# Routing of a slot mixture with phi as the stationary operand, four batch rows on the column groups, and slot sums from 32-row tiles

## The chip, the cores and the metric

One core of one Trainium2 chip runs the whole program. The metric is the device time of one execution in microseconds (us). Matrix products run on TensorE (PE; its weight loads are listed apart as PEld), elementwise work and reductions on VectorE (DVE), ScalarE (ACT) and GpSimd (POOL), and transfers are issued by SyncE (SP) for the most part.

## The reference

A gated delta rule over 768 tokens, for 4 batch rows and 8 heads of 48, is followed by a soft mixture over 32 slots. Its output, laid out as x of 3072 tokens by 384, is what the second part reads:

```python
logits = x @ phi                                  # 3072 x 32
d = np.exp(logits - logits.max(0, keepdims=True))
d /= d.sum(0, keepdims=True) + 1e-09              # over the tokens
slot_input = d.T @ x                              # 32 x 384
...
for e in range(E):                                # 8 experts, 4 slots each
    h = np.maximum(slot_input[e] @ w1[e], 0.0)
    slot_out[e] = h @ w2[e]
...
c = np.exp(logits - logits.max(1, keepdims=True))
c /= c.sum(1, keepdims=True) + 1e-09              # over the slots
return c @ slot_out
```

## The kernel before, in words

Tokens go in 24 chunks of 32. Four chunks are a group (index n, 6 groups), and a chunk has eight units: one batch row b (4) and one half g of the heads (2). A unit lies on the 128 partitions as four heads of 32 tokens each.

For each group, `norm` (L177) normalises the keys, `prep` (L204) transposes keys and queries and makes the small products, and `invert` (L240) inverts a triangular matrix for all 128 blocks of the group at once. The inversion is a strict chain on DVE: 31 steps of a product (L264) and a subtraction (L267). It starts when `lb` has come back from DRAM and POOL has scaled it (L252), and its result goes out through DRAM (L272) and comes back as weights `TT` (L282).

`chunk` (L298) is the recurrence: R = V - Kn S (products L310, difference L314), the inverse times R (L324, scaled on DVE in L329), the state's update (L340, L345) and the output Y (L354, L359, copied by ACT in L362).

`route(n, Yn)` (L370) takes a finished group through the mixture's first half. Its steps are

- `logits(b)`, for each batch row: four transposes of Y (L379), a copy by ACT to `yT` (L381), four accumulated products with `yT` (96 x 128) stationary and `phi` (96 x 32) moving (L385), and a copy to `lg` (L387);
- `over_slots`: the softmax over the slots, kept in `Call`;
- `maximum`: the running maximum over the tokens, by a transpose (L407), reductions, and a product that spreads it over the partitions (L415), then the exponential `d`;
- `sums`: the running sum of the exponentials, and the rescaling of both running sums;
- `repeat`: `d` spread over the four heads of a unit by four products with `sel` (L443), copied by ACT to `dr` (L448);
- `slots(c)`, for each chunk: POOL masks `dr` into `db` (L453, one instruction for each batch row), four products with Y stationary (128 x 96) and `db` moving (128 x 128) (L458), and an addition to `sacc` (L464).

These steps are handed to the next group's chunks: the first two chunks of group n carry `prep` of group n + 1, the last two carry `invert` of group n + 1 and `route` of group n - 1, in pieces between the chunk's own products (`Fill`, `merge`). A scheduler then sets the final order on each engine, and each engine keeps its order strictly. A matrix product in 32-bit floats shows as two records in the trace, a transpose as one.

After the last group its routing runs alone (`drain(routing)`, L529), and then the experts: `first` (L557, w1 stationary, `sacc` moving), `second` (L568, w2 moving), and the output (L588).

Of the kernel before, what the change touches and what calls it, by code (L numbers as in the profile page):

```python
# [16 lines left out]
def kernel(  # L17
# [85 lines left out]
    # the same by blocks: partition 32 h + 8 c + u of a group of chunks  # L103
# [30 lines left out]
    sel = cpool.tile([P, GC, 4, C], F32, name="sel")  # L134
    for h in range(4):
        nc.gpsimd.tensor_copy(sel[:, :, h, :], ident.rearrange("p (c t) -> p c t", t=C))
    ones = cpool.tile([P, 1], F32, name="ones")
    nc.vector.memset(ones, 1.0)
# [65 lines left out]
    def prep(n, c):  # L204
        """Of a chunk: Kn and Q transposed, strict_lower(Q Kn^T) and Kn Kn^T (both transposed)."""
# [34 lines left out]
    def invert(n):  # L240
        """(I + L)^-1 transposed: tt[block][k][i] = T[i, k], a block on each partition."""
# [34 lines left out]
    def near(cc):  # L276
        """Of the next chunk: its inverse as weights, and Kn spread by heads."""
# [87 lines left out]
    Call = cpool.tile([P, NG, B, NSL], F32, name="Call")  # L365
    dsum = cpool.tile([P, NSL], F32, name="dsum")
    sacc = cpool.tile([GD, 4, NSL], F32, name="sacc")
    mrun = cpool.tile([NSL, 1], F32, name="mrun")
    mB = {}

    def route(n, Yn):
# [30 lines left out]
        def maximum():  # L402
            # the running maximum over the tokens, on every partition
            cm = small.tile([P, NSL], F32, name="cm", tag="cm")
            nc.vector.tensor_reduce(cm, lg.rearrange("p b s -> p s b"), axis=AX.X, op=ALU.max)
            pm = pt([NSL, P])
            nc.tensor.transpose(pm, cm, ident)  # L407
            if n == 0:
                nc.vector.tensor_reduce(mrun, pm, axis=AX.X, op=ALU.max)
            else:  # L410
                m1 = small.tile([NSL, 1], F32, name="m1", tag="m1")
                nc.vector.tensor_reduce(m1, pm, axis=AX.X, op=ALU.max)
                nc.vector.tensor_tensor(mrun, mrun, m1, op=ALU.max)
            pmb = pt([P, NSL])
            nc.tensor.matmul(pmb, lhsT=mrun.broadcast_to([NSL, P]), rhs=ident[0:NSL, 0:NSL],  # L415
                             start=True, stop=True)
            mB[n] = small.tile([P, NSL], F32, name="mB", tag="mB")
            nc.vector.tensor_copy(mB[n], pmb)
            nc.vector.tensor_tensor(d, lg, mB[n].unsqueeze(1).broadcast_to([P, B, NSL]),
# [3 lines left out]
        def sums():  # L423
            if n == 0:
                nc.vector.tensor_reduce(dsum, d.rearrange("p b s -> p s b"), axis=AX.X,
                                        op=ALU.add)
                return
            al = small.tile([P, NSL], F32, name="al", tag="al")
            nc.vector.tensor_tensor(al, mB.pop(n - 1), mB[n], op=ALU.subtract)
            nc.scalar.activation(al, al, ACT.Exp)  # L430
# [192 lines left out]
```

## Time and profile before

| | |
|---|---|
| median of 3 runs | 919.21 us (918.97 to 921.51) |
| span of the profiled execution | 919.5 us |
| PE busy | 679.9 us, 74% of the span, 8324 instructions |
| PEld busy | 565.6 us |
| DVE busy | 299.4 us, 33% |
| POOL busy | 192.9 us, 21% |
| ACT busy | 101.3 us, 11% |
| mean granted clock of TensorE | 0.701 of full speed |

The profiled execution's own time is listed only as its span, 0.3 us above the median. Busy times are unions, so products that run beside each other count once. The page's line for the granted clock shows full speed up to 277 us, but the same products take as long there as later at half speed: that line is to be trusted from the first recorded change on.

### The profile page before, as it was taken

The numbers are of one execution on the slowest core, as the hardware profiler recorded it, in microseconds if no ns is written. First come the engines' busy times: TensorE is split into PE (matmuls) and PEld (weight loads), VectorE is DVE, ScalarE is ACT, GpSimd is POOL, SyncE is SP. The second block draws the span as 40 slices with busy tenths as digits, with TensorE's granted clock in tenths as the row PEclk, the third lists the DMA queues.
The fourth block names the chain that finished last, engine by engine and source line by source line (L and its number), as shares of the span: only waits on it lengthen the run. The fifth ranks groups of instructions, "written<-read, shape, count | busy, mean of one in ns | idle before, by whom it ended". The sixth has DMA issues, their size and how long they took to land.

```text
span 919.5 us, 19108 instructions
## 1 busy us (share of the span) xinstructions
PE 679.9 (74%) x8324; PEld 565.6 (62%) x8324; DVE 299.4 (33%) x816; ACT 101.3 (11%) x223; POOL 192.9 (21%) x347
## 2 busy tenths in 40 slices
PE   1706569069990799807998069996499799999998
PEld 1504569058880688706888058885398696765754
DVE  3267112942139421394213942226421100000011
ACT  0303000021120211102111021111000110000001
POOL 7231213131251213412134111351210200000000
PEclk9999999999995555755557555565555567667765
DMA  6240763023310242102321021000100099990013
GB/s 118 37 85 26 133 115 72 1 52 55 75 20 0 58 70 55 20 0 58 69 55 19 0 58 32 25 2 0 35 13 1 1 266 211 237 231 16 1 60 146
DMA packets 148019, 58.12 MB, mean 63 GB/s; under 512 B 131968, under 2 KB 143328, under 8 KB 147936
## 3 DMA queue, kind: packets, MB, share of 16 engines
q1 hardware_dynamic: 141888, 55.87, 27.9%
q10 hardware_dynamic: 5664, 0.94, 0.6%
q8 instruction: 65, 1.06, 0.5%
q0 software_dynamic: 384, 0.10, 0.1%
q14 instruction: 18, 0.15, 0.1%
HBM read 45.86 MB, written 11.01 MB: 62 GB/s over the span
## 4 chain that ended last, share of the span: by engine, by line
PE 64%; DVE 17%; DMA 6%; POOL 4%; SPq 3%; ACT 3%; issue 2%; ACTq 0%; DVEq 0%; POOLq 0%
PE ph L557 9%; PE psW L324 8%; PE psY L359 7%; DVE pr L264 7%; PE pso L568 6%; PE psS L340 6%; DVE tt L267 6%; PE pt L215 5%; PE pt L385 5%; PE pt L458 3%; PE pout L588 3%; PE psR L310 2%; PE pt L230 2%; PE psY L354 2%; PE pt L379 2%; SPq L77 2%
## 5 line engine op out<-in xcount | busy, mean ns | idle before, releaser
L215 PE MATMUL pt<-ident,Ks 128*128 128x128 f32 x96 | 42.1, 438 | 167.9 <-POOL Ks L199 158.7
L291 POOL TENSOR_TENSOR KX<-Ks,hm 128x192 f32<-128x192 f32 x184 | 91.0, 531 | 354.0 <-PE psS L340 264.4
L215 PEld LDWEIGHTS pt<-ident,Ks 128*128 128x128 f32 x96 | 20.8, 216 | 173.9 <-POOL Ks L199 159.6
L324 PE MATMUL psW<-R,TT 128*128 128x48 f32 x384 | 86.6, 396 | 34.4 <-DMA TT<-td 31.2
L324 PEld LDWEIGHTS psW<-R,TT 128*128 128x128 f32 x384 | 81.1, 311 | 39.4 <-DMA TT<-td 19.1
L557 PEld LDWEIGHTS ph<-sacc,w1t 96*128 96x128 f32 x512 | 87.8, 272 | 3.8 <-issue 3.8
L557 PE MATMUL ph<-sacc,w1t 96*128 96x4 f32 x512 | 88.1, 310 | 0.0
L359 PE MATMUL psY<-U,AT 128*128 128x48 f32 x384 | 83.9, 393 | 0.0
L264 DVE TENSOR_TENSOR pr<-tt,lb 128x31 f32<-128x31 f32 (+15 forms) x186 | 76.7, 413 | 16.2 <-POOL lb L252 11.0
L359 PEld LDWEIGHTS psY<-U,AT 128*128 128x128 f32 x384 | 78.2, 306 | 3.4
L267 DVE TENSOR_TENSOR tt<-tt,pr 128x31 f32<-128x31 f32 (+15 forms) x186 | 73.3, 394 | 5.2
L340 PE MATMUL psS<-U,KX 128*48 128x48 f32 x1472 | 69.8, 271 | 0.0
L340 PEld LDWEIGHTS psS<-U,KX 128*48 128x48 f32 x1472 | 60.8, 181 | 6.3 <-issue 1.7
L568 PE MATMUL pso<-w2t,hx 128*32 128x384 f32 x128 | 58.5, 627 | 1.7 <-DVE hx L561 1.7
L329 DVE TENSOR_TENSOR U<-psW,bta 128x192 f32<-128x192 f32 x48 | 17.2, 358 | 113.4 <-PE psW L324 113.4
L345 DVE TENSOR_TENSOR S<-S,psS 112x384 f32<-112x384 f32 x46 | 25.5, 554 | 87.6 <-PE psS L340 87.3
L233 DVE TENSOR_TENSOR AT<-pt,bdm 128x512 f32<-128x512 f32 x48 | 31.9, 688 | 62.1 <-ACT Lc L232 59.0
L385 PE MATMUL pt<-phi,yT 96*128 96x32 f32 x192 | 45.1, 398 | 6.0 <-ACT yT L381 5.1
L230 PE MATMUL pt<-KQ 48*32 48x64 f32 x1536 | 47.5, 310 | 1.9
L385 PEld LDWEIGHTS pt<-phi,yT 96*128 96x128 f32 x192 | 42.0, 323 | 10.5 <-ACT yT L381 9.1
L561 DVE TENSOR_SCALAR hx<-ph 128x32 f32<-128x32 f32 x8 | 1.5, 192 | 141.0 <-PE ph L557 141.0
L354 PE MATMUL psY<-S,KQ 48*32 48x48 f32 x1536 | 46.1, 265 | 0.1
(107 smaller groups left out, 698.9 us busy)
## 6 DMA issues: line engine op xcount, KB each, us to landing
w1t<-in_moe_w_dram SPq DMA_DIRECT2D x16, 768.0 KB
w2t<-in_moe_w_dram SPq DMA_DIRECT2D x8, 1536.0 KB
Ks<-in_k_dram SPq DMA_DIRECT2D x96, 48.0 KB
V<-in_v_dram SPq DMA_DIRECT2D x96, 48.0 KB
out_dram<-ob SPq DMA_DIRECT2D x24, 192.0 KB
Qs<-in_q_dram SPq DMA_DIRECT2D x80, 48.0 KB
ld<-Lc SPq DMA_DIRECT2D x24, 128.0 KB
lb<-ld SPq DMA_DIRECT2D x6, 512.0 KB
```

Source lines behind the costliest of these rows:

```text
L215: nc.tensor.transpose(tp[:, i, a, :], src[:, c, b * G:(b + 1) * G, :].rearrange("p g d -> p (g d)"), ident)
L230: nc.tensor.matmul(pg[rh, b], lhsT=KQ[cc][r, b, 0, rh], rhs=KQ[cc][r, b, :, rh], start=True, stop=True, skip_group_check=True)
L264: nc.vector.tensor_tensor(prv, tt[:, 0:m, j:j + 1].broadcast_to([P, m, w]), lb[:, j, j + 1:C].unsqueeze(1).broadcast_to([P, m, w]), op=ALU ...
L267: nc.vector.tensor_tensor(tt[:, 0:m, j + 1:C], tt[:, 0:m, j + 1:C], prv, op=ALU.subtract)
L291: nc.gpsimd.tensor_tensor(KX[cc][:, g, b], kn[:, b].unsqueeze(1).broadcast_to([P, 4, D]), hm.unsqueeze(2).broadcast_to([P, 4, D]), op=ALU. ...
L324: nc.tensor.matmul(pw[:, i, g, :], lhsT=T[:, (2 * hf + i) * G + g].rearrange("p h t -> p (h t)"), rhs=Rs[hf][:, i, g, :], start=True, stop ...
L340: nc.tensor.matmul(psS[DP * g:DP * g + D, i, h, :], lhsT=kx[:, g, 2 * hf + i, h, :], rhs=Us[hf][:, i, g, :], start=True, stop=True, skip_g ...
L354: nc.tensor.matmul(py[C * h:C * h + C, b, :], lhsT=kq[r, b, 1, C * h:C * h + C], rhs=old[b // 2][r, b % 2, h, :], start=(b == 0), stop=Fal ...
L359: nc.tensor.matmul(py[:, b, :], lhsT=at[:, g, b].rearrange("p h t -> p (h t)"), rhs=Us[b // 2][:, b % 2, g, :], start=False, stop=True, sk ...
L385: nc.tensor.matmul(pl, lhsT=yT[:, h].rearrange("p c t -> p (c t)"), rhs=phi[:, h, :], start=(h == 0), stop=(h == 3))
L557: nc.tensor.matmul(st["ph"][:, t, :], lhsT=w1t[e][:, h, t * P:(t + 1) * P], rhs=sacc[:, h, sl], start=(h == 0), stop=(h == 3))
L568: nc.tensor.matmul(pso, lhsT=hx[:, e, t, :], rhs=w2t[e][:, t, :], start=(e == 0 and t == 0), stop=(e == E - 1 and t == NFC - 1))
```

## The change

The routing is written anew. `turn(b)` does the transposes and the copy to `yT`, which now holds all four batch rows. One step `logits` follows: `phi` (96 x 32) is stationary, `yT` of one batch row and head (96 x 128) moves, and batch row b writes to partitions 32 b to 32 b + 31; a copy by ACT and one transpose bring the result back to tokens on the partitions. `maximum` makes the running maximum on all 128 partitions (four copies of the 32 slots), and with it the factor `al`, one number for each partition. `repeat` uses slices of the identity, 16 products with 32 columns of weights. `slots(c)` needs no masked copy: for each batch row and head, `dr` (32 x 32) of the head's own 32 partitions is stationary and Y of these partitions moves, with a column of ones behind its 96 columns, so that column 96 of `sacc` is the sum of the exponentials. `sums` and `sel` are gone; the two buffers of Y have four more columns, set to one at the start. Behind the last routing, `sacc` is transposed once to `sT` for the experts.

```diff
-        def logits(b):
+        def turn(b):
+            if b == 0:
+                st["yT"] = wk.tile([GD, B, 4, GC, C], F32, name="yT", tag="yT", bufs=1)
             py = pt([GD, GC, P])
             for c in range(GC):
-                nc.tensor.transpose(py[:, c, :], Yn[:, c, b, :], ident)
-            yT = wk.tile([GD, 4, GC, C], F32, name="yT", tag="yT")
-            nc.scalar.activation(yT.rearrange("p h c t -> p c h t"),
+                nc.tensor.transpose(py[:, c, :], Yn[:, c, b, 0:GD], ident)
+            nc.scalar.activation(st["yT"][:, b].rearrange("p h c t -> p c h t"),
                                  py.rearrange("p c (h t) -> p c h t", h=4), ACT.Copy)
-            pl = pt([P, NSL])
+
+        def logits():
+            pl = pt([P, P])
             for h in range(4):
-                nc.tensor.matmul(pl, lhsT=yT[:, h].rearrange("p c t -> p (c t)"),
-                                 rhs=phi[:, h, :], start=(h == 0), stop=(h == 3))
-            nc.vector.tensor_copy(lg[:, b, :], pl)
+                for b in range(B):
+                    nc.tensor.matmul(pl[C * b:C * b + C], lhsT=phi[:, h, :],
+                                     rhs=st["yT"][:, b, h].rearrange("p c t -> p (c t)"),
+                                     start=(h == 0), stop=(h == 3), skip_group_check=True)
+            lT = wk.tile([P, P], F32, name="lT", tag="lT", bufs=1)
+            nc.scalar.activation(lT, pl, ACT.Copy)
+            pq = pt([P, P])
+            nc.tensor.transpose(pq, lT, ident)
+            nc.vector.tensor_copy(lg.rearrange("p b s -> p (b s)"), pq)
...
         def maximum():
...
-            nc.tensor.transpose(pm, cm, ident)
+            nc.tensor.transpose(pm, cm.rearrange("p h s -> p (h s)"), ident)
...
+                nc.vector.tensor_tensor(al, mrun, m1, op=ALU.subtract)
+                nc.scalar.activation(al, al, ACT.Exp)
...
-            nc.vector.tensor_tensor(d, lg, mB[n].unsqueeze(1).broadcast_to([P, B, NSL]),
+            nc.vector.tensor_tensor(d, lg, pmb.unsqueeze(1).broadcast_to([P, B, NSL]),
                                     op=ALU.subtract)
...
-        def sums():
...
         def repeat():
             pd = pt([P, GC, B, NSL])
             for c in range(GC):
-                nc.tensor.matmul(pd[:, c].rearrange("p b s -> p (b s)"),
-                                 lhsT=sel[:, c].rearrange("p h t -> p (h t)"),
-                                 rhs=d.rearrange("p b s -> p (b s)"), start=True, stop=True,
-                                 skip_group_check=True)
+                for h in range(4):
+                    nc.tensor.matmul(pd[C * h:C * h + C, c].rearrange("p b s -> p (b s)"),
+                                     lhsT=ident[:, C * c:C * c + C],
+                                     rhs=d.rearrange("p b s -> p (b s)"), start=True, stop=True,
+                                     skip_group_check=True)
...
         def slots(c):
-            db = wk.tile([P, B, 4, NSL], F32, name="db", tag="db")
+            pa = pt([P, GD + 1])
             for b in range(B):
-                nc.gpsimd.tensor_tensor(
-                    db[:, b], st["dr"][:, c, b].unsqueeze(1).broadcast_to([P, 4, NSL]),
-                    hm.unsqueeze(2).broadcast_to([P, 4, NSL]), op=ALU.mult)
-            pa = pt([GD, 4, NSL])
-            for b in range(B):
-                nc.tensor.matmul(pa.rearrange("p h s -> p (h s)"), lhsT=Yn[:, c, b, :],
-                                 rhs=db[:, b].rearrange("p h s -> p (h s)"),
-                                 start=(b == 0), stop=(b == B - 1))
+                for h in range(4):
+                    r = slice(C * h, C * h + C)
+                    nc.tensor.matmul(pa[r], lhsT=st["dr"][r, c, b, :], rhs=Yn[r, c, b, 0:GD + 1],
+                                     start=(b == 0), stop=(b == B - 1), skip_group_check=True)
             if n == 0 and c == 0:
                 nc.vector.tensor_copy(sacc, pa)
+            elif c == 0:
+                nc.vector.scalar_tensor_tensor(sacc, sacc, st["al"], pa, op0=ALU.mult,
+                                               op1=ALU.add)
             else:
                 nc.vector.tensor_tensor(sacc, sacc, pa, op=ALU.add)
...
+    Ys = [wk.tile([P, GC, B, GD + 4], F32, name=f"Y{i}", bufs=1) for i in range(2)]
+    for t in Ys:
+        nc.gpsimd.memset(t[:, :, :, GD:GD + 4], 1.0)
...
+    pst = pt([GD, P])
+    nc.tensor.transpose(pst, sacc[:, 0:GD], ident)
+    sT = cpool.tile([GD, 4, NSL], F32, name="sT")
+    nc.vector.tensor_copy(sT.rearrange("p h s -> p (h s)"), pst)
```

The order on the engines moves as follows. First, PE in the third chunk of a middle group, before (L340 is the state's update of the third chunk, L354 and L359 its output):

```order
L340 MATMUL psS<-U,KX 48x48
L385 MATMUL pt<-phi,yT 128x32 x4
L379 MATMUL pt<-ident,Y 96x128 x4
L340 MATMUL psS<-U,KX 48x48 x13
L385 MATMUL pt<-phi,yT 128x32 x4
L340 MATMUL psS<-U,KX 48x48 x2
L379 MATMUL pt<-ident,Y 96x128 x4
L354 MATMUL psY<-S,KQ 32x48 x8
L340 MATMUL psS<-U,KX 48x48 x7
L385 MATMUL pt<-phi,yT 128x32 x4
L340 MATMUL psS<-U,KX 48x48 x9
```

and in the changed kernel, where L335 is the state's update, L375 the transposes, L384 the logits and L390 the transpose behind them:

```order
L335 MATMUL psS<-U,KX 48x48 x16
L375 MATMUL pt<-ident,Y_629 96x128 x4
L384 MATMUL pt<-yT,phi 32x128 x3
L335 MATMUL psS<-U,KX 48x48 x7
L384 MATMUL pt<-yT,phi 32x128 x13
L335 MATMUL psS<-U,KX 48x48 x8
L390 MATMUL pt<-ident,lT 128x128
L335 MATMUL psS<-U,KX 48x48
```

The logits of the four batch rows, spread over the chunk before, stand together, in two pieces. From the first transpose to the fourth chunk's first product the order before lists 38 rows, the changed one 32.

Second, PE from the routing's maximum to the fourth chunk (L324), before (L415 spreads the maximum, L443 repeats, L458 sums the slots):

```order
L415 MATMUL pt<-ident,mrun 128x32
L310 MATMUL psR<-S,KQ 32x48 x15
L354 MATMUL psY<-S,KQ 32x48 x22
L443 MATMUL pt<-d,sel 128x128 x4
L354 MATMUL psY<-S,KQ 32x48 x7
L458 MATMUL pt<-db,Y 96x128 x16
L324 MATMUL psW<-R,TT_213 128x48 x8
```

and in the changed kernel (L426 spreads, L437 repeats, L449 sums, L319 begins the fourth chunk):

```order
L349 MATMUL psY<-S,KQ 32x48 x28
L426 MATMUL pt<-ident,mrun 128x32
L349 MATMUL psY<-S,KQ 32x48 x3
L437 MATMUL pt<-d,ident 32x128 x16
L449 MATMUL pt<-Y_629,dr 32x97 x64
L319 MATMUL psW<-R,TT_206 128x48 x8
```

Less of the chunk's own work stands between the spreading and the repetition, and none between the repetition and the sums. The elimination steps follow behind the fourth chunk on DVE in both orders.

Third, DVE in the last group's inversion, where the routing of the group before it is threaded through the elimination steps, before (L464 adds the slot sums):

```order
L464 TENSOR_TENSOR sacc<-sacc,pt 96x128
L267 TENSOR_TENSOR tt<-tt,pr 128x19x13
L264 TENSOR_TENSOR pr<-tt,lb 128x240
L464 TENSOR_TENSOR sacc<-sacc,pt 96x128
L267 TENSOR_TENSOR tt<-tt,pr 128x20x12
L264 TENSOR_TENSOR pr<-tt,lb 128x231
L464 TENSOR_TENSOR sacc<-sacc,pt 96x128
```

and in the changed kernel:

```order
L454 SCALAR_TENSOR_TENSOR sacc<-sacc,al,pt 128x97
L259 TENSOR_TENSOR pr<-tt,lb 128x240
L262 TENSOR_TENSOR tt<-tt,pr 128x20x12
L457 TENSOR_TENSOR sacc<-sacc,pt 128x97
L259 TENSOR_TENSOR pr<-tt,lb 128x231
L262 TENSOR_TENSOR tt<-tt,pr 128x21x11
L457 TENSOR_TENSOR sacc<-sacc,pt 128x97
```

The additions stand at the same elimination steps. Ahead of them the four copies of the logits have become one, further down among the steps.

## Rows read from the trace of the kernel before

**Rows 1.** The page's chain of waits, by engine and by line.

```profile
PE 64%; DVE 17%; DMA 6%; POOL 4%; SPq 3%; ACT 3%; issue 2%; ACTq 0%; DVEq 0%; POOLq 0%
PE ph L557 9%; PE psW L324 8%; PE psY L359 7%; DVE pr L264 7%; PE pso L568 6%; PE psS L340 6%; DVE tt L267 6%; PE pt L215 5%; PE pt L385 5%; PE pt L458 3%; PE pout L588 3%; PE psR L310 2%; PE pt L230 2%; PE psY L354 2%; PE pt L379 2%; SPq L77 2%
```

**Rows 2.** Timeline of PE, 384 to 505 us: start, duration, instruction, wait ahead.

```profile
419.02 0.47 PE L215 MATMUL pt<-ident,Ks 128*128 128x128 f32 x1 [29.49 <-POOL Ks L199]
```

**Rows 3.** Timeline of DVE, the same stretch.

```profile
389.24 1.29 DVE L264 TENSOR_TENSOR pr<-tt,lb 128x31 f32<-128x31 f32 x1
...
419.32 0.21 DVE L267 TENSOR_TENSOR tt<-tt,pr 128x31 f32<-128x31 f32 x1
...
504.64 1.29 DVE L264 TENSOR_TENSOR pr<-tt,lb 128x31 f32<-128x31 f32 x1
```

**Rows 4.** Timeline of POOL, the same stretch.

```profile
495.73 1.91 POOL L252 TENSOR_TENSOR lb<-lb,bb 128x1024 f32<-128x1024 f32 x1
```

**Rows 5.** Timeline of PE, 440 to 505 us.

```profile
440.08 0.60 PE L310 MATMUL psR<-S,KQ 48*32 48x48 f32 x32
440.42 0.73 PE L230 MATMUL pt<-KQ 48*32 48x64 f32 x16
...
446.09 1.88 PE L230 MATMUL pt<-KQ 48*32 48x64 f32 x60
...
454.17 3.65 PE L359 MATMUL psY<-U,AT 128*128 128x48 f32 x16
...
473.37 0.40 PE L340 MATMUL psS<-U,KX 128*48 128x48 f32 x4
473.70 1.09 PE L379 MATMUL pt<-ident,Y 128*96 128x128 f32 x4
...
475.20 0.87 PE L340 MATMUL psS<-U,KX 128*48 128x48 f32 x14
476.00 1.92 PE L385 MATMUL pt<-phi,yT 96*128 96x32 f32 x8
477.85 1.04 PE L340 MATMUL psS<-U,KX 128*48 128x48 f32 x18
...
487.16 2.08 PE L443 MATMUL pt<-d,sel 128*128 128x128 f32 x8
489.17 0.54 PE L354 MATMUL psY<-S,KQ 48*32 48x48 f32 x14
490.46 6.58 PE L458 MATMUL pt<-db,Y 128*96 128x128 f32 x32 [0.76 <-POOL db L453]
496.88 0.99 PE L324 MATMUL psW<-R,TT 128*128 128x48 f32 x8
...
500.20 1.99 PE L359 MATMUL psY<-U,AT 128*128 128x48 f32 x16
```

**Rows 6.** Windows of PE: us, busy (records), granted clock, DMA share, GB/s.

```profile
496.00:497.00 1.00, 1.00 (x10) 0.83 0.00 0
...
736.00:738.00 2.00, 1.77 (x18) 1.00 0.28 25
...
742.00:744.00 2.00, 2.00 (x12) 0.52 1.06 399
```

**Rows 7.** Timeline of DVE, 617 to 656 us, the last inversion.

```profile
626.03 0.19 DVE L387 COPY lg<-pt 128x32 f32<-128x32 f32 x1 [0.67 <-PE pt L385]
...
633.11 0.19 DVE L387 COPY lg<-pt 128x32 f32<-128x32 f32 x1 [2.19 <-PE pt L385]
...
643.86 0.28 DVE L464 TENSOR_TENSOR sacc<-sacc,pt 96x128 f32<-96x128 f32 x1 [2.37 <-PE pt L458]
...
648.89 0.28 DVE L464 TENSOR_TENSOR sacc<-sacc,pt 96x128 f32<-96x128 f32 x1 [0.81 <-PE pt L458]
```

**Rows 8.** Timeline of PE, 700 to 742 us, the last routing.

```profile
714.55 1.92 PE L385 MATMUL pt<-phi,yT 96*128 96x32 f32 x8 [0.74 <-ACT yT L381]
...
730.41 6.09 PE L458 MATMUL pt<-db,Y 128*96 128x128 f32 x32 [1.23 <-POOL db L453]
```

More of the change, by code (lines that the diff above doesn't have):

```diff
@@ L133 @@
     nc.vector.tensor_tensor(bdm, bdm, hm.unsqueeze(2).broadcast_to([P, 4, C]), op=ALU.mult)
[L134 to L138, printed above, removed]
     bta = cpool.tile([P, NCH, U], F32, name="bta")
@@ L365 @@
     Call = cpool.tile([P, NG, B, NSL], F32, name="Call")
[L366 to L369, printed above, removed]
+    sacc = cpool.tile([P, GD + 1], F32, name="sacc")
+    mrun = cpool.tile([P, 1], F32, name="mrun")
     def route(n, Yn):
@@ L410, in maximum @@
             else:
-                m1 = small.tile([NSL, 1], F32, name="m1", tag="m1")
+                m1 = small.tile([P, 1], F32, name="m1", tag="m1")
+                al = st["al"] = small.tile([P, 1], F32, name="al", tag="al")
                 nc.vector.tensor_reduce(m1, pm, axis=AX.X, op=ALU.max)
-                nc.vector.tensor_tensor(mrun, mrun, m1, op=ALU.max)
+                nc.vector.tensor_tensor(m1, mrun, m1, op=ALU.max)
+                nc.vector.tensor_tensor(al, mrun, m1, op=ALU.subtract)
+                nc.scalar.activation(al, al, ACT.Exp)
+                nc.vector.tensor_copy(mrun, m1)
             pmb = pt([P, NSL])
[L415 to L418, printed above, removed]
-            nc.vector.tensor_tensor(d, lg, mB[n].unsqueeze(1).broadcast_to([P, B, NSL]),
+            nc.tensor.matmul(pmb, lhsT=mrun[0:NSL].broadcast_to([NSL, P]),
+                             rhs=ident[0:NSL, 0:NSL], start=True, stop=True)
+            nc.vector.tensor_tensor(d, lg, pmb.unsqueeze(1).broadcast_to([P, B, NSL]),
                                     op=ALU.subtract)
             nc.scalar.activation(d, d, ACT.Exp)
-        def sums():
[L424 to L430, printed above, removed]
-            ds_ = small.tile([P, NSL], F32, name="ds_", tag="ds_")
-            nc.vector.tensor_reduce(ds_, d.rearrange("p b s -> p s b"), axis=AX.X, op=ALU.add)
-            nc.vector.tensor_tensor(dsum, dsum, al, op=ALU.mult)
-            nc.vector.tensor_tensor(dsum, dsum, ds_, op=ALU.add)
-            nc.vector.tensor_tensor(sacc, sacc,
-                                    al[0:GD].unsqueeze(1).broadcast_to([GD, 4, NSL]),
-                                    op=ALU.mult)
         def repeat():
@@ L450, in slots @@
         def slots(c):
-            db = wk.tile([P, B, 4, NSL], F32, name="db", tag="db")
+            pa = pt([P, GD + 1])
             for b in range(B):
-                nc.gpsimd.tensor_tensor(
-                    db[:, b], st["dr"][:, c, b].unsqueeze(1).broadcast_to([P, 4, NSL]),
-                    hm.unsqueeze(2).broadcast_to([P, 4, NSL]), op=ALU.mult)
-            pa = pt([GD, 4, NSL])
-            for b in range(B):
-                nc.tensor.matmul(pa.rearrange("p h s -> p (h s)"), lhsT=Yn[:, c, b, :],
-                                 rhs=db[:, b].rearrange("p h s -> p (h s)"),
-                                 start=(b == 0), stop=(b == B - 1))
+                for h in range(4):
+                    r = slice(C * h, C * h + C)
+                    nc.tensor.matmul(pa[r], lhsT=st["dr"][r, c, b, :], rhs=Yn[r, c, b, 0:GD + 1],
+                                     start=(b == 0), stop=(b == B - 1), skip_group_check=True)
             if n == 0 and c == 0:
                 nc.vector.tensor_copy(sacc, pa)
+            elif c == 0:
+                nc.vector.scalar_tensor_tensor(sacc, sacc, st["al"], pa, op0=ALU.mult,
+                                               op1=ALU.add)
             else:
                 nc.vector.tensor_tensor(sacc, sacc, pa, op=ALU.add)
-        return ([lambda b=b: logits(b) for b in range(B)] + [over_slots, maximum, sums, repeat]
+        return ([lambda b=b: turn(b) for b in range(B)] + [logits, over_slots, maximum, repeat]
                 + [lambda c=c: slots(c) for c in range(GC)])
@@ L537 @@
         load_w2(e, wp2, 5)
-    pd = pt([NSL, 1])
-    nc.tensor.matmul(pd, lhsT=dsum, rhs=ones, start=True, stop=True)
     rd = cpool.tile([NSL, 1], F32, name="rd")
-    nc.vector.tensor_scalar(rd, pd, 1e-9, None, op0=ALU.add)
+    nc.vector.tensor_scalar(rd, sacc[0:NSL, GD:GD + 1], 1e-9, None, op0=ALU.add)
+    pst = pt([GD, P])
+    nc.tensor.transpose(pst, sacc[:, 0:GD], ident)
+    sT = cpool.tile([GD, 4, NSL], F32, name="sT")
+    nc.vector.tensor_copy(sT.rearrange("p h s -> p (h s)"), pst)
     nc.vector.reciprocal(rd, rd)
@@ L557, in product @@
                 nc.tensor.matmul(st["ph"][:, t, :], lhsT=w1t[e][:, h, t * P:(t + 1) * P],
-                                 rhs=sacc[:, h, sl], start=(h == 0), stop=(h == 3))
+                                 rhs=sT[:, h, sl], start=(h == 0), stop=(h == 3))
         def relu():
```

11 lines of the change are left out of this document (7 added, 4 removed).

## The prediction

> **What bounds the kernel now.** I read the chain of waits first [rows 1]: two thirds of it are PE, and DVE's part is nearly all the inversion (L264, L267). The timelines show how the two alternate. In a middle group, PE stands still for 29.49 us until the keys are normalised [rows 2]. In that time DVE runs the inversion's steps, from 389.24 to 419.32 us [rows 3], with the normalisation queued among them. The next inversion starts at 504.64, 115.4 us after the one before. So a period is 30 us of DVE, and 85 us in which PE works through four chunks, the next group's `prep` and the routing, strictly in its order. When does the inversion start? Its input `lb` is ready on POOL at 495.73 + 1.91 = 497.64 us [rows 4], 7.0 us ahead of its first step. It waits for its place in DVE's queue, behind the differences R that follow PE's fourth chunk. What PE saves in the routing therefore moves the inversion forward, one for one, up to those 7 us (and `lb` stands behind the masks L453 on POOL, which go away).
>
> This holds four times (routing of groups 0 to 3). The routing of group 4 runs beside the last inversion, the routing of group 5 alone: six calls in all, with different worth.
>
> **The unit prices.** PE runs at half its clock in most of this; the prices are for that. A product of 48 x 32 weights with 64 columns moving, four of them on the four column groups, comes every 31 ns per record (1.88 us for 60), so 0.49 ns per moving column [rows 5]. That gives 62 ns per record for 128 columns and 47 for 97; I take 60 and 45, since the last record's tail is in the 1.88. The two row groups of L310 even run beside each other: its 32 records have started within 0.34 us [rows 5].
>
> **The four calls on the path, part by part** (a call is one group's routing):
>
> - Transposes and their copies: the same 16, nothing.
> - Logits: four blocks of 8 records, 1.85 us each (476.00 to 477.85) [rows 5], 7.2 us with the shorter ones. Now 16 products, 32 records at 60 ns: 1.9 us. **-5.3.** The bound above is one column group after another: 32 records at the 0.25 us of L443, which also moves 128 columns, 8 us, so +0.8.
> - The copy by ACT and the transpose back: PE has eight products of L335 between, so the copy is covered; the transpose adds about a fourth of the four at 473.70, 0.3 us. **+0.3.** Without that cover the copy's 0.3 to 0.5 us come on top.
> - From the spread maximum to `d`: only three products of the chunk are left to cover a subtraction and an exponential (second place in the order); before, 37 were. **+0.6**, bounded by 0 and the 1.0 us that a round over DVE and ACT costs where nothing covers it.
> - Repetition: 2.01 us before (487.16 to 489.17) [rows 5], now 32 records at 60 ns. **-0.1.**
> - Slot sums: 6.42 us and 0.76 us of waiting for POOL [rows 5]. Now 128 records at 45 ns are 5.8 us; the wait for ACT's copy stays, without the hop over POOL but without the 0.54 us of L354 that covered it, so 0.8. **-0.6.** Bounds: 128 records at the 23 ns of a doubled clock are 2.9 us; with weight loads that don't hide, a third more, 7.7.
> - Fewer cuts: four records of L340 in a piece by themselves take 0.33 us (473.37 to 473.70), and 0.057 each in the piece of 14 at 475.20 [rows 5], so 0.1 for a cut. The order has 38 pieces before and 32 after. **-0.6.**
> - POOL's 96 masks and DVE's `sums` cost nothing on this path (DVE waits for PE there), so leaving them out gains nothing either.
>
> The sum is -5.7 a call; four calls **-23**.
>
> A rule speaks against the logits and the repetition. The row first: the 60 records of L230 stand on the same 48 partitions and differ in the column group alone, and they come every 31 ns [rows 5]. The Trainium skill ("TensorE: Matmul & The Clock Gate", Part 3, The mechanism) says that a weight load overlaps running products only where the row group differs. By that rule both blocks, whose 16 products share all their rows, would take 8 us at the 0.25 us of L443, and a call would lose 6.5 us in place of winning 5.7. The trace disagrees with it, so the sum goes by the row.
>
> **The call beside the last inversion.** Here DVE is the path, and it waits for PE between its steps: eight waits, from 0.67 us at 626.03 to 0.81 at 648.89, the longest 2.19 and 2.37, 9.1 us together [rows 7], since the logits' copies and the slot sums stand among the steps. After the change PE has all 16 transposes in a row and one block of logits, about 8 us, while DVE has ten steps to do, about 7.5 us: that wait nearly goes. Those for the maximum, `d` and the slots stay, about 4 us. **-5** (bounds -1 and -8).
>
> **The last call alone.** Everything counts. Before, from 714.55 on, each batch row's products wait 0.74 us for their copy [rows 8]; three such waits become one (-1.5), logits -5.3, the slots' wait 1.23 to 0.75 and 0.3 less work (-0.8); the copy and transpose back add 0.8, the transpose of `sacc` about what the sum over `dsum` took. **-6.5** (bounds -4 and -8).
>
> In all -34.5.
>
> **The clock.** The page's stretch of full speed is where the sums can go wrong. The clock rises at 496.2 us, 5.7 us into L458 [rows 6], and falls once PE has stood still. So the fourth chunk runs at full speed: 16 records of L359 take 1.92 us there against 3.58 in the second chunk [rows 5]. At half speed the 8.0 us from 496.88 on would be about 13: the rise is worth 5 us in each of four groups, and as much at the end, where the last L458 raises the clock up to 742 us [rows 6]. All five rises up to there lie in this block. Its successor has another shape and is 0.6 us shorter. I take that the clock rises in it too, but one time in five too late, since a block of 5.8 us barely reaches the 5.7 us after which that rise came: +5.
>
> **Forecast:** 919.5 - 34.5 + 5 = 890 us; the median lies 0.3 below this execution, so 890 on the runs' scale too.
>
> **Rivals.**
>
> 1. *The clock stays at half speed in the routing.* For it: the rise at 496.2 comes late in the block, and no tiled block of this trace is followed by one. Against it: no tiled block here is as long. The rises of four groups and of the end are lost: 919.5 - 34.5 + 25 = 910 us.
> 2. *The slots' row tiles take turns, and the kernel gets slower.* The four products of a round write one PSUM bank from four row groups. No row shows that: L310's two row groups write two banks. If they took turns, a record would come every 180 ns, and a call's slots would take 23 us at half speed; with the clock rising after 5.7 us, 14.4, or 8.6 more than I count. Six calls: 919.5 - 34.5 + 52 = 937 us, over 1000 with the clock lost as well. It decides from 34.5 / 768 records = 45 ns more per record, so from 90 ns; with the clock lost from 57 ns. The Trainium skill ("TensorEngine Tiling (Array Packing)", Gotcha 1: PSUM Pressure) says that different row tiles cannot access the same bank at one time and that software must see to it. It gives no time; if the hardware did it, this rival would hold.
> 3. *The change gains only alone.* If `lb` held the inversion, only the last two calls would count: 919.5 - 11.5 = 908. Against it: the 7.0 us of slack.
> 4. *The column groups take turns*, at the upper bound of logits and repetition: 6.5 us lost in each of six calls, 919.5 + 39 + 5 = 964 us. Against it: the 31 ns of L230.
>
> **How the numbers follow.** Forecast 0.58, rival 1 0.24, rival 2 0.10, rival 3 0.04, rival 4 0.02; 0.02 for no effect at all. What a measurement of this kernel can tell from no change is about 0.3%, 2.8 us. The forecast, rival 3 and nearly all of rival 1 (with its slots at 54 ns and a wait more it ends within the bound) are faster: 0.83. Same 0.05, slower (rivals 2 and 4) 0.12. The forecast alone holds 877 to 903; up to 914 the range takes in rival 1, and rivals 2 and 4 are left out.
>
> **What would show it.** L384 near 60 ns per record and L449 near 45; PE's wait for the keys still near 30 us, with periods of about 110 us; a granted clock of 1.0 behind L449; DVE's waits in the last inversion down to 4 us. It is wrong if L449 takes over 11 us a call, if a new wait of over 1 us stands ahead of L390, L437 or L449, or if a middle group's inversion begins with a wait for POOL.

## The result and the profile after

The changed kernel takes 869.0 us (median of 4 runs, 860.5 to 871.7) against 920.4 us: ratio 0.943 [0.938, 0.948]. Two more measurements gave 873.9 us, 0.948 [0.945, 0.951], and 864.9 us, 0.940 [0.938, 0.943]. So it is faster, as forecast, but by 48 to 55 us, not 30, and all three medians lie below the range.

The page of the changed kernel, its span, busy times and chain:

```profile
span 858.6 us, 20412 instructions
PE 618.6 (72%) x9049; PEld 507.6 (59%) x9049; DVE 292.3 (34%) x782; ACT 102.6 (12%) x229; POOL 156.6 (18%) x249
PE 66%; DVE 18%; DMA 6%; POOL 3%; ACT 3%; issue 2%; SPq 2%; ACTq 0%; DVEq 0%; POOLq 0%
PE ph L556 10%; PE psW L319 9%; PE psY L354 8%; DVE pr L259 7%; PE psS L335 7%; PE pso L567 7%; DVE tt L262 6%; PE pt L210 5%; PE pout L587 3%; PE pt L449 3%; PE pt L225 3%; PE psY L349 3%; PE pt L375 3%; DMA TT<-td 3%; PE psR L305 2%
```

PE has lost 61 us of busy time, as many as the span; the logits, at 5% of the chain before [rows 1], are no longer in the list.

The timeline of PE in a middle group, call 1, from the second chunk's first product (321.74) to the fourth's (360.37); the first two lines are from the kernel before, the second chunk's first product, to go with the fourth's at 496.88 [rows 5], and a block of its logits:

```profile
447.90 1.94 PE L324 MATMUL psW<-R,TT 128*128 128x48 f32 x8
...
459.73 1.91 PE L385 MATMUL pt<-phi,yT 96*128 96x32 f32 x8
```

```profile
321.74 1.94 PE L319 MATMUL psW<-R,TT 128*128 128x48 f32 x8
...
341.89 0.65 PE L384 MATMUL pt<-yT,phi 96*32 96x128 f32 x6
342.47 0.88 PE L335 MATMUL psS<-U,KX 128*48 128x48 f32 x14
343.28 1.42 PE L384 MATMUL pt<-yT,phi 96*32 96x128 f32 x26
344.63 0.56 PE L335 MATMUL psS<-U,KX 128*48 128x48 f32 x16
345.13 0.33 PE L390 MATMUL pt<-ident,lT 128*128 128x128 f32 x1
...
346.08 1.09 PE L354 MATMUL psY<-U,AT 128*128 128x48 f32 x8
347.10 0.55 PE L349 MATMUL psY<-S,KQ 48*32 48x48 f32 x32
347.57 1.09 PE L354 MATMUL psY<-U,AT 128*128 128x48 f32 x8
...
350.98 0.63 PE L426 MATMUL pt<-ident,mrun 32*128 32x32 f32 x2 [0.52 <-DVE mrun L424]
...
352.33 1.94 PE L437 MATMUL pt<-d,ident 128*32 128x128 f32 x32 [0.41 <-ACT d L430]
355.05 5.40 PE L449 MATMUL pt<-Y,dr 32*32 32x97 f32 x128 [0.78 <-ACT dr L442]
360.37 1.43 PE L319 MATMUL psW<-R,TT 128*128 128x48 f32 x8
```

The prices are those of the forecast: L384 (0.65 + 1.42)/32 = 65 ns per record in two pieces, L437 1.94/32 = 61, L449 5.40/128 = 42, and the waits are 0.5, 0.4 and 0.8 us. Still, the stretch has shrunk from 49.0 us (447.90 to 496.88 before) to 38.6, so by 10.3 us and not by 5.7. Windows (us, busy and records, granted clock), first of the third chunk before, then of the stretch above:

```profile
470.00:490.00 20.00, 19.43 (x293) 0.50 0.03 6
```

```profile
336.00:344.00 8.00, 8.00 (x89) 0.50 0.54 112
344.00:351.00 7.00, 6.48 (x241) 0.99 0.01 2
351.00:355.00 4.00, 2.86 (x40) 0.50 0.34 63
...
361.00:371.50 10.50, 7.54 (x223) 0.99 0.01 3
```

The clock rises *twice* in this call: as before behind the slots (361 us), and for 7 us ahead of the maximum, here within the new logits. I call the second one the early rise. Before, none of calls 1 to 3 has it. The early rise does not need the new logits in front of it. In call 1 of the third execution of the table below it starts 4 us ahead of their first product:

```profile
335.00:336.00 1.00, 1.00 (x37) 0.76 0.29 60
```

```profile
335.61 1.09 PE L319 MATMUL psW<-R,TT 128*128 128x48 f32 x8
...
339.60 0.42 PE L384 MATMUL pt<-yT,phi 96*32 96x128 f32 x6
```

What PE's order lacks ahead of that rise, against before and transposes apart, is the block of old logits shown above (L385 at 459.73).

By stage, in us of the profiled executions, cut at the fourth chunk's second product (the row that waits 0.45 us for U), for call 3 at the end of the slots. The first and the third execution of the changed kernel are the shortest of their measurements (860.5 and 859.3 us, against medians of 869.0 and 864.9):

| stage | before | changed, first | second | third | old logits, new slots |
|---|---|---|---|---|---|
| to group 0's fourth chunk | 150.7 | 152.1 | 151.9 | 151.8 | 152.5 |
| to the next, with call 0 | 117.4 | 104.6 | 107.2 | 105.6 | 116.2 |
| with call 1 | 114.8 | 105.6 | 105.0 | 100.9 | 114.7 |
| with call 2 | 115.4 | 104.1 | 105.6 | 104.9 | 113.8 |
| with call 3 | 120.0 | 108.5 | 113.3 | 107.6 | 118.7 |
| last inversion | 45.3 | 40.2 | 40.3 | 40.2 | 46.5 |
| last call | 74.1 | 65.5 | 65.6 | 64.8 | 73.2 |
| experts, output | 181.7 | 178.1 | 181.2 | 181.6 | 178.2 |
| span | 919.5 | 858.6 | 870.1 | 857.4 | 913.9 |

### The profile page after: what moved, and what is told of

The parts are those of the page before. It is cut to its first block, busy times and chain, and to the rows that moved or that the text cites. A ratio compares the mean times of both kernels' runs of the same rounds, so it can differ in the third digit from the quotient of the medians.

```text
span 858.6 us, 20412 instructions
## 1 busy us (share of the span) xinstructions
PE 618.6 (72%) x9049; PEld 507.6 (59%) x9049; DVE 292.3 (34%) x782; ACT 102.6 (12%) x229; POOL 156.6 (18%) x249
## 4 chain that ended last, share of the span: by engine, by line
PE 66%; DVE 18%; DMA 6%; POOL 3%; ACT 3%; issue 2%; SPq 2%; ACTq 0%; DVEq 0%; POOLq 0%
PE ph L556 10%; PE psW L319 9%; PE psY L354 8%; DVE pr L259 7%; PE psS L335 7%; PE pso L567 7%; DVE tt L262 6%; PE pt L210 5%; PE pout L587 3%; PE pt L449 3%; PE pt L225 3%; PE psY L349 3%; PE pt L375 3%; DMA TT<-td 3%; PE psR L305 2%
## 5 line engine op out<-in xcount | busy, mean ns | idle before, releaser
L319 PE MATMUL psW<-R,TT 128*128 128x48 f32 x384 | 84.9, 391 | 33.8 <-DMA TT<-td 30.6
L319 PEld LDWEIGHTS psW<-R,TT 128*128 128x128 f32 x384 | 79.8, 307 | 39.4 <-DMA TT<-td 18.8
L556 PEld LDWEIGHTS ph<-sT,w1t 96*128 96x128 f32 x512 | 85.0, 265 | 3.8 <-issue 3.8
L556 PE MATMUL ph<-sT,w1t 96*128 96x4 f32 x512 | 85.4, 305 | 0.0
L354 PE MATMUL psY<-U,AT 128*128 128x48 f32 x384 | 77.5, 372 | 0.0
L354 PEld LDWEIGHTS psY<-U,AT 128*128 128x128 f32 x384 | 72.1, 285 | 3.0
L335 PE MATMUL psS<-U,KX 128*48 128x48 f32 x1472 | 66.0, 266 | 0.0
L335 PEld LDWEIGHTS psS<-U,KX 128*48 128x48 f32 x1472 | 58.0, 177 | 6.4 <-issue 2.3
L567 PE MATMUL pso<-w2t,hx 128*32 128x384 f32 x128 | 56.3, 608 | 1.7 <-DVE hx L560 1.7
L340 DVE TENSOR_TENSOR S<-S,psS 112x384 f32<-112x384 f32 x46 | 25.5, 555 | 91.0 <-PE psS L335 90.9
L324 DVE TENSOR_TENSOR U<-psW,bta 128x192 f32<-128x192 f32 x48 | 17.2, 358 | 113.1 <-PE psW L319 113.1
L225 PEld LDWEIGHTS pt<-KQ 48*32 48x32 f32 x1536 | 34.6, 154 | 14.9 <-ACT KQ L213 11.8
L349 PE MATMUL psY<-S,KQ 48*32 48x48 f32 x1536 | 40.5, 250 | 2.7 <-issue 2.6
L357 ACT ACTIVATE Y<-psY 128x192 f32<-128x192 f32 x48 | 15.9, 330 | 219.4 <-PE psY L354 219.4
```

Of the source, the lines that this page charges most:

```text
L225: nc.tensor.matmul(pg[rh, b], lhsT=KQ[cc][r, b, 0, rh], rhs=KQ[cc][r, b, :, rh], start=True, stop=True, skip_group_check=True)
L319: nc.tensor.matmul(pw[:, i, g, :], lhsT=T[:, (2 * hf + i) * G + g].rearrange("p h t -> p (h t)"), rhs=Rs[hf][:, i, g, :], start=True, stop ...
L335: nc.tensor.matmul(psS[DP * g:DP * g + D, i, h, :], lhsT=kx[:, g, 2 * hf + i, h, :], rhs=Us[hf][:, i, g, :], start=True, stop=True, skip_g ...
L349: nc.tensor.matmul(py[C * h:C * h + C, b, :], lhsT=kq[r, b, 1, C * h:C * h + C], rhs=old[b // 2][r, b % 2, h, :], start=(b == 0), stop=Fal ...
L354: nc.tensor.matmul(py[:, b, :], lhsT=at[:, g, b].rearrange("p h t -> p (h t)"), rhs=Us[b // 2][:, b % 2, g, :], start=False, stop=True, sk ...
L556: nc.tensor.matmul(st["ph"][:, t, :], lhsT=w1t[e][:, h, t * P:(t + 1) * P], rhs=sT[:, h, sl], start=(h == 0), stop=(h == 3))
```

## The experiments

**The changed kernel measured again** (no edit).

> The changed kernel, timed again. Theory A (clock): what it gained beyond the forecast, some 5 us in each middle group, is a second rise of TensorE's clock behind the block of logits, and single executions differ because the rises fall sometimes earlier, sometimes later: times between 858 and 873 us, and in the profile a granted clock of 1.0 between L384 and L426 in most groups. Theory B (work): the products themselves are shorter than priced, and the clock has no part in it: times within 0.5% of each other.

873.9 us, single executions 868.2 to 875.6, and the granted clock of theory A in calls 1 and 2. **A third time**, on another chip, beside later kernels:

> The changed kernel again, beside the three kernels below on the same chip: 869 to 874 us by its two measurements.

864.9 us, below what I expected. The three medians differ by 1%, more than before's (920.3 to 921.7); how much of that is the chip was not separated. The second execution of the table shows one reason: its call 3 lacks the early rise and takes 113.3 us where the other two take 107.6 and 108.5. Windows of it:

```profile
555.00:566.00 11.00, 11.00 (x179) 0.50 0.01 3
566.00:577.00 11.00, 11.00 (x175) 0.50 0.01 1
```

**Old logits in the changed kernel**, all else new.

```diff
-        return ([lambda b=b: turn(b) for b in range(B)] + [logits, over_slots, maximum, repeat]
+        return ([lambda b=b: logits(b) for b in range(B)] + [over_slots, maximum, repeat]
```

with `logits(b)` as in the kernel before.

> The new repetition, slot sums and maximum with the logits of the kernel before. Theory A: no rise of the clock in the third chunk; from the second chunk's first L319 to the fourth's it takes about 47 us (before 48.9, changed kernel 38.6); the whole about 908 us. Theory B: the extra 5 us a group come from the new slots and fewer cuts, so about 43 us for that stretch and about 890 us for the whole.

915.4 us, ratio 0.994 [0.992, 0.996], and 48.0 us for the stretch (333.74 to 381.73): theory A, even slower than it said. The new logits carry nearly all of the gain, 41.5 us; maximum, repetition and slots give 1.0 us a call. Its timeline and windows, the same place as above:

```profile
361.84 1.92 PE L379 MATMUL pt<-phi,yT 96*128 96x32 f32 x8
363.69 1.04 PE L335 MATMUL psS<-U,KX 128*48 128x48 f32 x18
...
364.96 1.94 PE L354 MATMUL psY<-U,AT 128*128 128x48 f32 x8
366.83 0.87 PE L349 MATMUL psY<-S,KQ 48*32 48x48 f32 x32
367.63 1.94 PE L354 MATMUL psY<-U,AT 128*128 128x48 f32 x8
```

```profile
329.50:354.00 24.50, 24.40 (x322) 0.50 0.45 88
354.00:364.00 10.00, 10.00 (x98) 0.50 0.03 7
364.00:376.00 12.00, 11.06 (x235) 0.50 0.12 23
```

From its start to the next instruction an old block takes 1.72 to 1.85 us (361.84 to 363.69 here), the four together 7.1; the two new pieces take 0.58 and 1.35 in the timeline above (2.4 together in the call without an early rise). That is 5.2 us less, the forecast's 5.3. The other gain is in the chunk's own products behind them, which the change did not touch: a block of L354 takes 1.87 us to the next instruction here and 1.02 in the changed kernel (346.08 to 347.10), a block of L349 0.80 and 0.47. Added up over the blocks to L426 I estimate 3.5 us. PE has no wait of 0.3 us or more from 329.5 to 373 us here and the clock stays at 0.50. The Trainium skill ("TensorE: Matmul & The Clock Gate", Part 1, What's actually happening) says that the clock is half by default and that activity releases it; these rows show 43 us of nearly unbroken work that did not.

**The new logits in four steps**, one for each head, to break up the block; `logits(h)` makes one head's products, and behind the last the copy and the transpose.

```diff
-        return ([lambda b=b: turn(b) for b in range(B)] + [logits, over_slots, maximum, repeat]
+        return ([lambda b=b: turn(b) for b in range(B)] + [lambda h=h: logits(h) for h in range(4)]
+                + [over_slots, maximum, repeat]
```

> The changed kernel with its logits as four steps, one for each head of a half, so that the 16 products stand in three or four pieces with the chunk's output products between. Same products, same tiles. Theory A: no rise of the clock ahead of L426, the stretch from the second chunk's first psW product to the fourth's takes about 44 us in place of 38.6, of which 1 us is a longer wait for the maximum; the whole is about 22 us slower than the changed kernel, near 890. Theory B: only the 1 us of waiting and two more cuts, some 5 us in all, near 874.

874.5 us, 0.948 [0.944, 0.952], near theory B's time, but with the early rise still there in calls 1 and 2 (352 to 362 us and 458 to 468), the first time behind 8 of the 32 records. The single dense block is not what matters; this reading of mine fell.

**Neighbours on one tile**: the loops over b and h swapped in logits and slots, so that products behind each other share their column group, or row tile and column group.

```diff
-            for h in range(4):
-                for b in range(B):
+            for b in range(B):
+                for h in range(4):
...
-            for b in range(B):
-                for h in range(4):
+            for h in range(4):
+                for b in range(B):
```

> The changed kernel with the loops of logits and slot sums turned round, so that four products in a row stand on the same column group (logits) or the same 32-row tile (slots). If the tiles run beside each other only when neighbours in the order differ: the logits' 32 records take about 6.8 us at half clock in place of 2.0 (the 0.25 us of a full product, less the load), the slots' 128 records some 20 us in place of 5.4. If the rate is set by the records themselves: 2.0 and 5.4 as before.

913.2 and 930.2 us in two runs, too few for an interval, but at least 37 us more than any run of the changed kernel. The records, of the longer one:

```profile
361.29 3.65 PE L384 MATMUL pt<-yT,phi 96*32 96x128 f32 x32
375.81 11.30 PE L449 MATMUL pt<-Y,dr 32*32 32x97 f32 x128 [0.78 <-ACT dr L442]
...
722.45 2.46 PE L384 MATMUL pt<-yT,phi 96*32 96x128 f32 x32
```

L449 takes 88 ns per record against 42, both at a granted 0.50. L384 takes 114 at 361 us, mostly at half clock: the products ahead of it take as long as at half speed, though the clock's line, before its first recorded change, shows 1.0. At 722 us, at full clock, it takes 77. Both stand against 65. The price is about half of what I expected for L449. So the tiles do run beside each other in the changed kernel, and the order of the loops alone is worth a factor of two on the slots. The order also cost the slots' rise: in calls 1 and 2 the fourth chunk stays at half clock (L354 at 392.76 takes 3.65 us, 1.99 in the changed kernel). A longer block of the same records, 11.3 us in place of 5.4, had no rise behind it.

**New products added to the old logits**: 16 of them (32 records) behind the fourth batch row's, then 48 (`range(3)`), results unread.

```diff
+        def extra():
+            pz = pt([P, P])
+            for _ in range(1):
+                for h in range(4):
+                    for b in range(B):
+                        nc.tensor.matmul(pz[C * b:C * b + C], lhsT=phi[:, h, :],
+                                         rhs=st["yT"][:, h].rearrange("p c t -> p (c t)"),
+                                         start=True, stop=True, skip_group_check=True)
```

> The changed kernel with the old logits (as in the run with the slots alone, 915.4 us), and behind the fourth batch row's logits 16 more products of the new form (weights 96x32, moving 128 columns, four column groups; 32 records), whose result nobody reads. Clock theory: what the new logits gave beyond their shorter work is a second rise of the granted clock in the third chunk; then these products bring it back although they add work: 32 records at 60 ns are 1.9 us a call, +7.7 us for four calls, and the rise gives up to 5 us in each of three middle groups, so 908 to 916 us, with a granted clock of 1.0 behind them, ahead of the products of the maximum. Work theory (the new logits and their copies were simply shorter than priced): no rise there, 915.4 + 7.7 = 923 us.

918.7 us, 0.998 [0.996, 1.000]: between the two expectations. Its profiled execution, 928.8 us, is the longest of twelve. It has no early rise in calls 1 to 3 (0.50 from 365 to 375 us, behind the added products); whether the shorter ones have one was not recorded.

> The same with 48 such products in place of 16 (96 records). Clock theory: the rise comes within them, so that their later ones cost half; 96 records at 60 to 30 ns are 2.9 to 5.8 us a call, 12 to 23 us for four, less 5 us or more in each middle group: 910 to 925 us, with a clear stretch at 1.0. Work theory: 915.4 + 23 = 938 us, no rise in the third chunk.

927.5 us, 1.007 [1.004, 1.010]: just above the clock theory's range, and 12 us more than with the old logits alone, where four calls add 4 x 5.1 = 20 us of records. Its row and windows:

```profile
364.07 5.12 PE L388 MATMUL pt<-yT,phi 96*32 96x128 f32 x96
```

```profile
364.00:369.00 5.00, 5.00 (x97) 0.52 0.00 0
369.00:376.00 7.00, 5.10 (x183) 0.98 0.02 6
```

The rise comes at the end of the added products, where the old logits by themselves have none; it lasts 7 us in calls 1 and 3 and 3 us in call 2. It gives back part of their cost, not all: a clock that is raised by work for its own sake lost more than it won here.

**A quarter of each form**: one head's logits in place of four, new form and old form. Both have 8 logits records a call. They differ in which operand is stationary, in the transpose back, and in the place: the new form's records stand together (349.19 to 350.52 us in call 1), the old form's in four pairs from 340.67 to 354.07.

```diff
-            for h in range(4):
+            for h in range(1):
```

> The changed kernel with the logits of one head in place of four (8 records in place of 32; the other three heads' products are left out). Two readings of the second rise of the clock. New products raise it: with a quarter of them no rise in the third chunk, 873.9 - 4 x 24 x 58 ns (5.6) + 3 x 4.4 = 881.5 us. Old products held it down: the rise stays at its place without them, some 1.4 us earlier, and the time is 873.9 - 5.6 = 868 us.

> The kernel with the old logits and the new slots (915.4 us), with one head's logits in place of four (2 records in place of 8 a batch row, 24 fewer a call at 239 ns: 5.7 us; the other three heads' products are left out). If the old products held the clock down, the rise now comes in the third chunk: 915.4 - 4 x 5.7 - 3 x 4.4 = 879 us. If the new products raise it, no rise there: 892.6 us.

870.4 us, 0.946 [0.943, 0.948], and 883.8 us, 0.961 [0.959, 0.963]. The first time is near "the old products held it down" (868). The second lies between the two readings (879 and 892.6), and its trace shows no early rise, so neither reading holds by itself. Windows of the new form in calls 1 and 2, then of the old form:

```profile
350.00:356.00 6.00, 6.00 (x220) 1.00 0.02 5
...
457.00:464.00 7.00, 7.00 (x177) 0.50 0.01 4
```

```profile
350.00:355.00 5.00, 5.00 (x59) 0.50 0.01 4
355.00:362.00 7.00, 6.82 (x164) 0.50 0.01 2
```

With 8 records of 96 x 32 weights and 128 moving columns the clock rises ahead of the maximum in call 1, and again in call 3 (561 to 568 us), not in call 2; with 8 records of 96 x 128 weights and 32 moving columns it does so in none of the three. Calls 1 and 2 take 104.7 and 107.0 us with the new form, 109.3 and 109.1 with the old. The products themselves account for about 1.2 us of that, 8 x (239 - 58) ns less 0.3 for the transpose back; so I estimate that the early rise is worth about 3.5 us in call 1 (against call 2 of the same execution, 2.3). In this pair the rise came in two of three calls with the one form and in none with the other. That does not show that the form decides. These are one execution of each; in call 1 of the new form the rise starts 0.4 us into its products; and the old form's profiled execution (888.7 us, mean granted clock 0.704) is 4 to 6 us longer than five of its seven runs, whose mean clock is 0.705 to 0.709, so those may have a rise that was not recorded. Why call 2 lacks it stays open too.

**Products that nobody reads while PE waits for the keys**: 96 (192 records), in the kernel before and in the changed one, then 132 in the changed one.

```diff
+    def warm():
+        pz = ps.tile([NSL, P], F32, name="pz", tag="psW")
+        for _ in range(96):
+            nc.tensor.matmul(pz, lhsT=phi[:, 0, :], rhs=phi.rearrange("p h s -> p (h s)"),
+                             start=True, stop=True, skip_group_check=True)
...
+            if c == 0 and 0 < n < NG - 1:
+                steps = [warm] + steps
```

> The kernel before with 96 products (weights 96x32, moving 128 columns, 192 records; nobody reads them) where TensorE waits 29.5 us for the scaled keys at the head of each middle group. At 115 ns a record they take at most 22 us and end ahead of the keys. If TensorE's clock is what the time goes by in the chunks, it is raised when the keys come: the transposes and products behind them run at 1.0 for some 7 to 11 us, as behind the other rises, 3.5 to 5.5 us saved in each of three groups: 905 to 911 us from 921. If the preparation there goes by VectorE's copies and masks, not by TensorE, 921 as before. If the products last longer than the wait, slower by what is over.

919.1 us, 0.999 [0.997, 1.001], no gain. Its rows show why:

```profile
274.67 20.71 PE L477 MATMUL pz<-phi 96*32 96x128 f32 x188
...
304.78 0.48 PE L215 MATMUL pt<-ident,Ks 128*128 128x128 f32 x1 [8.61 <-POOL Ks L199]
```

They ended 8.6 us ahead of the keys and the clock had fallen again (0.50 from 299 us). On one tile a record took 110 ns, although the granted clock was 1.0 from 274 to 299 us.

> The same 96 products in the changed kernel, in the same wait (28.4 us). If the clock decides: 3.5 to 5.5 us in each of three groups, 858 to 864 us from 873.9, faster than both kernels. If VectorE decides there: 874. Slower only if the products outlast the wait.

865.1 us, 0.941 [0.937, 0.945]. The "864" of the expectation seemed met, but the changed kernel's third measurement gave 864.9 without the added products, so no gain is shown here either. In call 1 of this run the early rise again starts 4 us ahead of the first new logits product (336.4 and 340.52).

> The changed kernel with 132 products that nobody reads in place of 96 in TensorE's wait for the keys (264 records at the 110 ns measured are 29.0 us in a wait of 28.4 us, 0.9 us of it other products): they last until the keys come. If the clock is what the next stretch goes by, it is at 1.0 when the 8 transposes and 64 products of the first two chunks begin, which then take some 1.1 us in place of 1.9 each; some 7 us at full clock give 3.5 us in each of three groups: 855 to 862 us beside 865 with 96. If the masks and copies on VectorE set the pace there, as their waits of 0.64 us suggest, about 866. Slower than 868 only if the products outlast the keys.

860.2 us, 0.933 [0.929, 0.937], against 864.9 for the changed kernel on the same chip, whose interval lies just above: 0.5% faster, the best kernel here. Its rows:

```profile
270.50 28.57 PE L470 MATMUL pz<-phi 96*32 96x128 f32 x260
...
300.64 0.33 PE L210 MATMUL pt<-ident,Ks 128*128 128x128 f32 x1 [0.79 <-POOL Ks L194]
...
301.99 1.26 PE L225 MATMUL pt<-KQ 48*32 48x64 f32 x64 [0.25 <-ACT KQ L213]
```

Eight transposes and the 64 products behind them (1.26 us, 1.90 in the changed kernel) run at full clock, then the clock falls. From the first transpose to the second chunk's first product it is 27.9 us (300.64 to 328.53) where the changed kernel needs 28.9 (293.58 to 322.51 in its third execution). That is 3 us in three groups; where the rest of the 4.7 came from was not traced.

## Why the prediction was right and wrong

**Right:** what bounds the kernel, the unit prices, and the work on the four calls' path (below). PE's savings moved the inversion forward one for one: the wait for the keys is 28.4 to 28.6 us, and `lb` is ready at 458.81, 13.9 us ahead of the inversion's first step, against 7.0 before [rows 4]:

```profile
456.90 1.91 POOL L247 TENSOR_TENSOR lb<-lb,bb 128x1024 f32<-128x1024 f32 x1
```

```profile
472.72 1.34 DVE L259 TENSOR_TENSOR pr<-tt,lb 128x31 f32<-128x31 f32 x1
```

Rival 2 fell: four row tiles write one bank at 42 ns per record. So the turns that the Trainium skill ("TensorEngine Tiling (Array Packing)", Gotcha 1: PSUM Pressure) led me to fear cost no time here. These four tiles also write four different sets of 32 partitions; row tiles that write the same partitions of a bank were not run. Rival 4 fell: L384's products share their 96 rows and come every 60 to 65 ns. The experiment with the loops in turn limits what falls: neighbours on the *same* column group did not overlap, so what the Trainium skill ("TensorE: Matmul & The Clock Gate", Part 3, The mechanism) requires of the row group, a different column group supplied here. Rival 1 fell: a rise at the slots came in each of calls 1 to 3 in all three executions, in calls 1 and 2 within or behind them, in call 3 as they began or up to 1.3 us ahead. Rival 3 is out by the stages: each of the four calls is 7 to 14 us shorter.

**The last inversion:** forecast -5, measured -5.1 to -5.2. DVE's waits in it:

```profile
577.81 0.19 DVE L259 TENSOR_TENSOR pr<-tt,lb 128x31 f32<-128x31 f32 x1 [2.63 <-POOL lb L247]
...
585.96 0.29 DVE L391 COPY lg<-pt 128x128 f32<-128x128 f32 x1 [1.09 <-PE pt L390]
589.56 0.29 DVE L420 TENSOR_REDUCE m<-pt 128x1 f32<-128x128 f32 x1 [0.22 <-PE pt L414]
591.88 0.29 DVE L428 TENSOR_TENSOR d<-lg,pt 128x128 f32<-128x128 f32 x1 [0.33 <-PE pt L426]
...
596.93 0.32 DVE L454 SCALAR_TENSOR_TENSOR sacc<-sacc,al,pt 128x97 f32<-128x97 f32 x1 [1.24 <-PE pt L449]
599.45 0.26 DVE L457 TENSOR_TENSOR sacc<-sacc,pt 128x97 f32<-128x97 f32 x1 [0.29 <-PE pt L449]
```

The waits among the steps are 3.2 us, where I expected 4 and [rows 7] had 9.1. Ahead of them this inversion waits 2.63 us for `lb`, where it waited 1.54 before (620.64): rival 3's mechanism, in the one place where it showed, and there already before the change.

**The last call:** forecast -6.5 (its parts add up to -6.8), measured -8.5 to -9.3. The sum took three of four waits for a copy to become one, -1.5. In the changed kernel none of 0.2 us or more is left: before they were 0.68 and three times 0.74, 2.9 us.

**Wrong, the step "The clock".** I put +5 there: one rise a call, behind the slots, which the new shape might miss one time in five. I counted what a new shape of products could take from the clock and not what taking the old ones away could give. With the new logits in place of the old a second rise of 7 us (once 10) comes in the third chunk, ahead of the maximum, in 8 of the 9 calls 1 to 3 of the three profiled executions, and the slots' rise stays. With the old logits and all else new it is gone. By the pair with one head I estimate 2.3 to 3.5 us for it; the call without it was 5 us longer. The reason that I gave for the +5 did not hold either: behind a block of 5.4 us the rise came, behind one of 11.3 us in the other order it did not.

The four calls by themselves, forecast -23 with 4 of the +5: about -19. Measured: -45, -37 and -49 us. The work is about 5.9 us a call, where I had 5.7: logits -5.2, plus 0.3 for the transpose back, and -1.0 for everything else (the run with the old logits). The rest, 3.2 to 6.3 us a call, I put down to the clock, with whatever the saved cuts among the logits give beyond that. So in the four calls the clock term was -13 to -25 us, not +4. That is nearly all of the 18 to 30 us by which these calls fell below the forecast, and most of the 20 to 33 us by which the three spans did (870.1, 858.6 and 857.4 against 890). The medians are only 16 to 25 us below it, since the first and the third of these executions are shorter than their medians.

What was not shown is why the early rise comes. Two readings are left. *The new products raise it*: for it, the rise behind 96 of them added to the old logits; against it, the rises that start 4 us ahead of the first of them, and the profiled execution with 32 added ones and no rise. *The old products held it down*: for it, those two; against it, the trace with a quarter of the old products and no rise. The runs show which instructions preceded a rise and which did not, no more.

Three slips in the working changed nothing. The 60 records of L230 lie on two sets of 48 rows, one for each g of `products(g)`, and not on one; L384 has since shown the same with one set. The rise before came at 496.3 us by the window in [rows 6] (0.83 of 496 to 497), so 5.9 us into L458 and not 5.7. And an execution's time lies 1.9 us above its span here (860.5 and 858.6), so the execution profiled before took about 921 us, 2 above the median; the forecast on the runs' scale is 890 by this way too.

## What to carry to other kernels

Count a change to TensorE's products twice, once for their own records and once for the clock behind them: look in the windows for what ran ahead of each rise, and ask of a change both which rises it takes and which it may bring. Order the loops so that neighbours lie on different tiles (42 against 88 ns per record here). When a gain is far larger than the sum of the removed records, compare unchanged products before and after, with the granted clock beside them: here a block of L354 went from 1.87 to 1.02 us as the clock went from 0.50 to 1.0. Where executions of one kernel differ by 1%, a gain of 1% needs more than one measurement.

## What the runs showed of the hardware

- PE without a wait of 0.3 us or more between 329.5 and 373 us (old logits) stayed at a granted 0.50 all the while.
- The early rises last about 7 us (344 to 351), once 10 (335.5 to 345.5). That one ended while PE had no wait (PE busy 2.41 of the 2.50 us from 345.5 to 348).
- One block of 128 records was followed by a rise in one order of its loops (5.40 us) and by none in another (11.30 us), in calls 1 and 2.
- Products on four row tiles of 32 that write one bank, each on its own 32 partitions, came every 42 ns at half clock (97 columns), on the same tile every 88 ns. A loop of products on one tile took 110 ns per record of 128 columns at full clock, 1.8 times the 60 ns that four column groups take at half.
